# Attention and feed-forward in one kernel: low parts of the input weights to GpSimd, new ranks, whole batches in order, seven groups behind the attention

## The chip, the cores and the metric

The kernel runs on one core of one Trainium2 chip. The metric is the device time of one execution in microseconds (us). The kernel before was run three times: 585.23, 585.49 and 589.45 us, so its median is 585.49 us. The engines are called PE (matrix multiply), DVE (vector), ACT (scalar), POOL (GpSimd) and SP (it issues most DMAs). Each works through its own queue in the order in which the program was built, and waits at an instruction until what it needs is there.

## What is computed

The reference is an attention over 4 batches of 8 heads (576 positions, head width 64) with a recurrent memory, followed by a feed-forward layer on the 2304 x 512 result, all in float32:

```
scores = where(causal, -1e9, q @ k.T / sqrt(D))
a      = exp(scores - rowmax);  a /= a.sum + 1e-9
qp     = phi(q) = where(q > 0, q, exp(q) - 1) + 1
x      = g * (qp @ M_prev) / (qp . z_prev + 1e-6) + (1 - g) * (a @ v)      g = sigmoid(beta)
h      = x @ w_in                  # 2304 x 512 by 512 x 2048
out    = (s * relu(h)**2 + b) @ w_out
```

## The kernel before

**The three stages.** First comes the attention, in 16 pairs of heads (four pairs to a batch), then what is left of the first product (x @ w_in), then the second product, which is made with Strassen's seven products out of 256-wide quarters. To keep float32 accuracy every operand of a product is split into a high part (H) and a low part (L), and a product is three matmuls: H by H, H by L, L by H. Lines 494 to 496 are these three for the first product, 705 to 707 for the second.

**A pair of heads** goes through: scores on PE (line 322) into the banks `sb`; the row maximum on DVE with the mask added (329, `red`), which also moves the scores to SBUF; the exponential on ACT (335); the reciprocal of the sums on DVE (366, 367); ten scalings on POOL (341); transposes on PE (391) into the banks `tb`; copies of these banks on ACT and DVE (401 to 408); the product with V on PE (434); and at its end x is split into `xs`, high part on ACT (455) and low part on DVE (456). The query's feature map (272 to 286) runs on ACT, DVE and POOL beside it. All buffers of a pair exist twice, so two pairs are in flight.

**The weights w_in** come as float64 words in 20 pieces: 8 small ones (256 columns) and 12 large ones (512 columns). Each is made into float32 by one step on ACT (480) and three on DVE (481, 482, 484); POOL then writes the high part (486) and DVE subtracts it for the low part (487).

**The first product** is cut into groups: batch b by 128 columns of w_in, f = 0 to 15, twelve matmuls of 512 columns each. A group can run as soon as the batch's four pairs and its pieces of w_in are done. Groups of batches 0, 1 and 2 (48 of them) fill PE between the attention's steps; a ReLU on ACT (514) and a DMA to HBM (515) take each result out. Batch 3 and the 256 leftover columns of all batches (called batch 4) come behind the attention: there PE's results land in `hps`, one of 8 PSUM banks, go through the ReLU of line 500 into `r` and by DMA (501) to HBM.

**What sets the order.** Up to the end of the attention the order of every engine is written by a planner (`Plan`, lines 42 to 143): each step has an engine, an assumed cost and a rank, and of the steps that are ready the one of lowest rank goes first. On PE a group of the first product goes on until attention work has been ready for `HOLD` us or amounts to `WORK` us. Behind the attention the work is written step by step: `t_mm1` makes half a group, `tick` counts, and `later(n, ...)` hangs other work n ticks behind. That other work is the conversion of w_out in 16 pieces (`conv_u`, `t_u`, `split_u`, lines 604 to 634), the start of the second product's left operand (`g_load`, `g_make`, `operand`) and the ReLU with its DMA. A scheduler may still move these instructions on DVE, ACT and POOL.

## Time and profile before

| | before |
|---|---|
| three runs, us | 585.23, 585.49, 589.45 |
| profiled execution, us | 584.89 |
| its span, first to last instruction, us | 583.1 |
| PE busy | 546.6 us, 94% |
| ACT busy | 396.6 us, 68% |
| DVE busy | 367.9 us, 63% |
| POOL busy | 307.1 us, 53% |

The profiled execution's time is 1.8 us more than its span: that is what lies around the first and the last instruction. Its 584.89 us stand 0.6 us below the median. A busy share is an average over the stages, and it counts a slow or overlapped instruction as busy as well, so PE's 94% does not say that only 6% can be won. In the windows of the trace, a line gives for one stretch of the span the busy time of each engine with its instructions in brackets, then PE's granted clock (1.00 is 2.4 GHz, half of it 1.2 GHz) and the share and speed of the DMAs.

### The profile page before, as it was taken

Reading aid. Unit: us, or ns where it says so; the run is one execution under the profiler, and the core shown is the slowest. Engines: PE = TensorE matmul, PEld = TensorE weight load, DVE = VectorE, ACT = ScalarE, POOL = GpSimd, SP = SyncE. Lnnn points to the kernel's source line nnn. Section 1 sums busy time; section 2 is a strip of 40 time slices with the busy share of each in tenths; the row PEclk is TensorE's granted clock in tenths of the full one; section 3 lists DMA queues with packets and bytes.
Section 4 is the critical chain, followed back from the end, with each engine's and each line's share of the span. In section 5 each row is a group of like instructions: output and inputs, shape, how many; then the busy total and the mean of one; then the engine's idle time right before and its main releaser. Section 6 shows DMA issues by size and latency. Waiting matters only on the chain.

```text
span 583.1 us, 11806 instructions
## 1 busy us (share of the span) xinstructions
PE 546.6 (94%) x4309; PEld 462.5 (79%) x4309; DVE 367.9 (63%) x884; ACT 396.6 (68%) x846; POOL 307.1 (53%) x325
## 2 busy tenths in 40 slices
PE   6986996899989999999999999987999999999997
PEld 4755764577768777777778888876999999999997
DVE  4889898787752156453210389689657866695561
ACT  4898877667643278766632457958897779777940
POOL 2699778757752046554300000044786688668750
PEclk9799899799999999999999999997999999999999
DMA  6635566356623234331112876727344344444011
GB/s 185 191 117 157 154 202 202 121 165 205 194 85 129 91 97 130 105 119 60 51 59 90 315 228 208 261 110 241 131 136 144 121 142 142 139 124 139 28 38 37
DMA packets 53354, 81.52 MB, mean 140 GB/s; under 512 B 7216, under 2 KB 32816, under 8 KB 53296
## 3 DMA queue, kind: packets, MB, share of 16 engines
q1 hardware_dynamic: 52144, 79.19, 42.4%
q10 hardware_dynamic: 1152, 1.57, 0.7%
q8 instruction: 34, 0.56, 0.4%
q14 instruction: 24, 0.20, 0.1%
HBM read 57.15 MB, written 23.59 MB: 138 GB/s over the span
## 4 chain that ended last, share of the span: by engine, by line
PE 68%; ACT 8%; DVE 7%; POOL 7%; DMA 6%; issue 3%; SPq 0%; ACTq 0%; POOLq 0%; DVEq 0%
PE yps L707 10%; PE yps L705 10%; PE yps L706 10%; PE tb L494 7%; PE sb L434 7%; PE tb L496 6%; PE tb L495 6%; PE sb L322 6%; DMA r_d<-r 5%; POOL P L341 5%; PE tb L391 4%; ACT P L335 2%; DVE P L329 2%; DMA raw<-in_moe_w_out_dram 1%; ACT r L500 1%
## 5 line engine op out<-in xcount | busy, mean ns | idle before, releaser
L341 POOL TENSOR_SCALAR P<-P,sm,omg 128x192 f32<-128x192 f32 (+4 forms) x160 | 114.7, 735 | 71.5 <-DVE sm L367 45.2
L707 PE MATMUL yps<-bH,op 128*128 128x256 f32 x360 | 102.2, 284 | 4.2 <-DVE op L697 4.2
L706 PE MATMUL yps<-bL,op 128*128 128x256 f32 x360 | 102.2, 284 | 0.1
L705 PE MATMUL yps<-bH,op 128*128 128x256 f32 x360 | 102.2, 284 | 0.0
L335 ACT ACTIVATE P<-P,mn 128x64 f32<-128x64 f32 (+4 forms) x160 | 88.5, 561 | 18.8 <-DVE mn L329 18.8
L691 POOL TENSOR_TENSOR sum<-w0L 128x512 f32<-128x512 f32 x20 | 34.6, 1734 | 121.2 <-DVE stg L203 92.2
L329 DVE CUSTOM_DVE_ANT_0 P<-sb,mask 128x320 f32<-128x320 f32 (+4 forms) x160 | 69.4, 483 | 32.7 <-PE sb L322 31.8
L707 PEld LDWEIGHTS yps<-bH,op 128*128 128x128 f32 x360 | 68.9, 192 | 4.4 <-DVE op L697 4.4
L706 PEld LDWEIGHTS yps<-bL,op 128*128 128x128 f32 x360 | 68.8, 191 | 0.3 <-DVE bL L634 0.3
L705 PEld LDWEIGHTS yps<-bH,op 128*128 128x128 f32 x360 | 68.9, 191 | 0.2 <-ACT bH L633 0.2
L322 PE MATMUL sb<-qk 64*128 64x288 f32 (+4 forms) x384 | 62.9, 437 | 5.3 <-DVE mn L329 4.4
L391 PEld LDWEIGHTS tb<-ident,P 64*128 64x128 f32 x928 | 41.0, 143 | 31.4 <-POOL P L286 7.7
L391 PE MATMUL tb<-ident,P 64*128 64x64 f32 x928 | 47.5, 233 | 17.4 <-POOL P L341 5.0
L514 ACT ACTIVATE r<-tb 128x512 f32<-128x512 f32 x48 | 28.5, 594 | 46.0 <-PE tb L496 41.2
L322 PEld LDWEIGHTS sb<-qk 64*128 64x128 f32 x384 | 41.7, 200 | 18.5 <-DVE mn L329 7.5
L401 ACT COPY pt<-tb 128x512 f32<-128x512 f32 x64 | 34.4, 594 | 18.2 <-PE tb L391 18.1
L697 POOL TENSOR_TENSOR op<-w0L,op 128x512 fp32r<-128x512 f32 x30 | 41.6, 1407 | 4.9 <-ACT op L696 4.7
L696 ACT CAST op<-w0L 128x512 fp32r<-128x512 f32 x50 | 30.2, 614 | 18.5 <-PE yps L707 11.3
L705 PE MATMUL yps<-w0H,op 128*128 128x256 f32 x144 | 40.7, 283 | 0.0
L706 PE MATMUL yps<-w1H,op 128*128 128x256 f32 x144 | 40.7, 283 | 0.0
L707 PE MATMUL yps<-w0H,op 128*128 128x256 f32 x144 | 40.7, 283 | 0.0
L494 PE MATMUL tb<-xs,w0H 128*128 128x512 f32 x96 | 40.6, 422 | 0.0
(135 smaller groups left out, 1428.6 us busy)
## 6 DMA issues: line engine op xcount, KB each, us to landing
r_d<-r SPq DMA_DIRECT2D x60, 256.0 KB, 2.0
w0L<-r_d SPq DMA_DIRECT2D x20, 512.0 KB, 4.8
qk<-in_qk_t_dram SPq DMA_DIRECT2D x15, 576.0 KB, 4.1
raw<-in_moe_w_out_dram SPq DMA_DIRECT2D x16, 512.0 KB, 5.1
w1L<-r_d SPq DMA_DIRECT2D x16, 512.0 KB, 4.4
xa<-in_moe_w_in_dram SPq DMA_DIRECT2D x12, 512.0 KB, 4.4
qs<-in_q_rows_dram SPq DMA_DIRECT2D x16, 320.0 KB, 3.8
V<-in_vm_dram SPq DMA_DIRECT2D x16, 256.0 KB, 2.7
```

Source lines behind the costliest of these rows:

```text
L322: nc.tensor.matmul(SB[ps[j]][:, o:o + n], lhsT=qk[rs, 128 * i:128 * i + 128], rhs=qk[rs, S + 64 + c0:S + 64 + c0 + n], start=True, stop=Tr ...
L329: nc.vector.tensor_tensor_reduce(P[:, j, PB[i] + 64:PB[i] + 64 + n], SB[ps[j]][:, o:o + n], m, -SCALE, 3.0e38, ALU.add, ALU.min, mn[:, j, ...
L335: nc.scalar.activation(pt, pt, AF.Exp, scale=-1.0, bias=mn[:, j, i:i + 1], accum_out=sm[:, j, i:i + 1])
L341: nc.gpsimd.tensor_scalar(pt, pt, sm[:, j, i:i + 1], omg[:, h:h + 1], ALU.mult, ALU.mult)
L391: nc.tensor.transpose(TB[ps[h]][:, o[h]:o[h] + 64], P[rs, j, c:c + 128], ident[rs, rs], tile_position=(64 * h, 0))
L434: nc.tensor.matmul(t[64 * j:64 * j + 64, off:], lhsT=V[:, c, j], rhs=rhs, start=k == 0, stop=k == len(steps[0]) - 1, tile_position=(0, 64 ...
L494: nc.tensor.matmul(ps, lhsT=wH[:, p, fs], rhs=xs[:, 0], start=p == 0, stop=False)
L495: nc.tensor.matmul(ps, lhsT=wH[:, p, fs], rhs=xs[:, 1], start=False, stop=False)
L697: (nc.gpsimd if m in ONPOOL else nc.vector).tensor_sub(L, x, H.bitcast(F32))
L705: nc.tensor.matmul(ps, lhsT=H, rhs=BH, start=f == 0, stop=False)
L706: nc.tensor.matmul(ps, lhsT=H, rhs=BL, start=False, stop=False)
L707: nc.tensor.matmul(ps, lhsT=L, rhs=BH, start=False, stop=f == KF - 1)
```

## The change

- The low part of w_in (the subtraction of line 487) goes from DVE to POOL for the first 16 of the 20 pieces; the last four stay on DVE.
- Ranks: the row maxima (by `UR`), the copies of the transposes' banks (by `UC`) and the split of x (by `UX`) are ranked earlier, that is, ahead of other work on DVE and ACT; the pieces of w_in get earlier ranks (the largest falls from 20.8 to 16.2). `HOLD` and `WORK` change from 1.5 and 1.0 to 1.0 and 2.0.
- The groups of the first product go by whole batches: all 16 of batch 0, then all 16 of batch 1, then nine of batch 2. Before, eight of batch 0 came first, then eight of batch 1, and then the other halves.
- Seven groups of batch 2 (f = 9 to 15) run behind the attention, ahead of batches 3 and 4.
- There the ReLU works in pieces of 256 columns with three buffers of one kind; before, one buffer held 512 columns and another 256. The DMA of a piece goes on ACT's queue for batch 2 and on SP's for the rest; before, on ACT's for f below 4.
- The conversion of w_out gets other ticks (`CT`), and the first operands of the second product come six ticks sooner behind their start.

```diff
-    SWITCH, HOLD, WORK = 0.14, 1.5, 1.0
+    SWITCH, HOLD, WORK = 0.14, 1.0, 2.0
...
-    rpool = p1.enter_context(tc.tile_pool(name="rpool", bufs=1))
+    rpool = p1.enter_context(tc.tile_pool(name="rpool", bufs=3))
...
+    UR, UC, UX = 0.6, 0.5, 1.0
...
             for k, (i, o) in enumerate(tiles):
-                    add("DVE", RED[i], lambda i=i, j=j, o=o, ps=ps: red(i, j, o, ps), r + 0.1 + 0.01 * k,
+                    add("DVE", RED[i], lambda i=i, j=j, o=o, ps=ps: red(i, j, o, ps), r + 0.1 + 0.01 * k - UR,
...
             for h in range(2):
-                    r + 0.1, [("tp", g, k)], [("pt", u if k > 1 else 2, h, k)], give=[(ps, h, "T")])
+                    r + 0.1 - UC, [("tp", g, k)], [("pt", u if k > 1 else 2, h, k)], give=[(ps, h, "T")])
...
                 w = 0.16 + 0.00085 * (z - a)
-                add("ACT", w, lambda t=t, d=d: nc.scalar.copy(d[:, 0], t()), r0 + 2.3, [("av", g)], key(0))
+                add("ACT", w, lambda t=t, d=d: nc.scalar.copy(d[:, 0], t()), r0 + 2.3 - UX, [("av", g)], key(0))
-                    r0 + 2.3, [("av", g)] + key(0), key(1),
+                    r0 + 2.3 - UX, [("av", g)] + key(0), key(1),
...
         add("POOL", 0.8, lambda: nc.gpsimd.tensor_scalar(H, w, 1.0, 1.0, ALU.mult, ALU.mult), rank, [B_], [("WH", n)])
-        add("DVE", 0.8, lambda: nc.vector.tensor_sub(L, w, H.bitcast(F32)), rank, [B_, ("WH", n)], [("WL", n)])
+        low = ("POOL", 1.35, nc.gpsimd) if n < WP else ("DVE", 0.8, nc.vector)
+        add(*low[:2], lambda: low[2].tensor_sub(L, w, H.bitcast(F32)), rank, [B_, ("WH", n)], [("WL", n)])
...
     def mm1_out(b, f, ps):
-        r = rpool.tile([128, COLS[b]], F32, tag=f"r{b // B}", name="r")
-        nc.scalar.activation(r, ps, AF.Relu)
-        (nc.scalar if f < 4 else nc.sync).dma_start(r_d[b][:, f], r)
+        for o in range(0, COLS[b], 256):
+            r = rpool.tile([128, 256], F32, tag="r", name="r")
+            nc.scalar.activation(r, ps[:, o:o + 256], AF.Relu)
+            (nc.scalar if b == 2 else nc.sync).dma_start(r_d[b][:, f, o:o + 256], r)
...
-    FSPLIT = 8
-    MM = [(b, f) for r in (range(0, FSPLIT), range(FSPLIT, NF)) for b in range(2) for f in r] + [(2, f) for f in range(NF)]
-    STAGE = [b if m < FSPLIT or b == 2 else 1 for m, (b, f) in enumerate(MM)]
-    WB, WS = 12.0, 0.8
-    WRANK = [6.5, 6.6, 7.0, 7.2] + [9.0, 9.1, 9.2, 9.3] + [WB + WS * k for k in range(12)]
+    LEFT = 7
+    MM = [(b, f) for b in range(B - 1) for f in range(NF - LEFT * (b == 2))]
+    WP = 16
+    WRANK = [5.0, 6.6, 7.0, 7.2] + [9.0 + 0.2 * k for k in range(4)] + [10.0 + 0.2 * k for k in range(4)] + [
+        12.0 + 0.6 * k for k in range(8)]
...
             for m in range(len(MM)):
-                if STAGE[m] == g // NP:
+                if MM[m][0] == g // NP:
     with tc.manual_schedule():
-    MM = [(b, f, half) for f in range(NF) for b in (B, B - 1) for half in range(2)]
+    MM = [(2, f, half) for f in range(NF - LEFT, NF) for half in range(2)]
+    MM += [(b, f, half) for f in range(NF) for b in (B, B - 1) for half in range(2)]
     pa.close()
...
-    CT0, CT1 = 1, 3
+    CT = [1, 3, 6, 8, 10, 13] + [15 + 3 * k for k in range(10)]
...
-        later(CT0 + CT1 * i, conv_u, i)
+        later(CT[i], conv_u, i)
     while MM:
...
                 later(LT + i, g_make, 0, i)
-                later(max(LT + 4 + i, begin + CT0 + CT1 * (4 * i + 3) + 5 - clock[0]), late_b, i, 0)
+                later(max(LT + 4 + i, begin + CT[4 * i + 3] + 5 - clock[0]), late_b, i, 0)
-                later(LT + 14 + i, operand, 0, SEQ[i // 2], i % 2)
+                later(LT + 8 + i, operand, 0, SEQ[i // 2], i % 2)
```

The order of POOL near the seventh pair (the scalings of one pair and the feature map of the next; `w_106` and `w_107` are the two buffers of a piece of w_in, `w0H`, `w1H`, `w0L`, `w1L` its high and low parts). Before:

```order
L486 TENSOR_SCALAR w0H<-w_107 128x512
L341 TENSOR_SCALAR P_121<-P_121,sm_119,omg 128x576 x2
L486 TENSOR_SCALAR w0H<-w_106 128x512
L341 TENSOR_SCALAR P_122<-P_122,sm_120,omg 128x448
L486 TENSOR_SCALAR w0H<-w_107 128x512
L341 TENSOR_SCALAR P_122<-P_122,sm_120,omg 128x448
L341 TENSOR_SCALAR P_122<-P_122,sm_120,omg 128x192 x2
L276 TENSOR_TENSOR phr<-qs_114,z_112 128x640
L341 TENSOR_SCALAR P_122<-P_122,sm_120,omg 128x320 x2
L341 TENSOR_SCALAR P_122<-P_122,sm_120,omg 128x64 x2
L486 TENSOR_SCALAR w1H<-w_106 128x512
L286 TENSOR_TENSOR P_122<-qs_114,nrm_116 128x3x2x64
```

With the change:

```order
L487 TENSOR_SCALAR w0H<-w_106 128x512
L342 TENSOR_SCALAR P_121<-P_121,sm_119,omg 128x448
L489 TENSOR_TENSOR w0L<-w_106,w0H 128x512
L487 TENSOR_SCALAR w0H<-w_107 128x512
L342 TENSOR_SCALAR P_121<-P_121,sm_119,omg 128x192
L489 TENSOR_TENSOR w0L<-w_107,w0H 128x512
L342 TENSOR_SCALAR P_121<-P_121,sm_119,omg 128x192
L277 TENSOR_TENSOR phr<-qs_113,z_111 128x640
L487 TENSOR_SCALAR w1H<-w_106 128x512
L342 TENSOR_SCALAR P_121<-P_121,sm_119,omg 128x320
L489 TENSOR_TENSOR w1L<-w_106,w1H 128x512
L342 TENSOR_SCALAR P_121<-P_121,sm_119,omg 128x320
```

The low parts (489) now stand in POOL's queue, and the casts of the high parts (487) stand earlier by some pairs, both between the single scalings (342).

The order of PE where the attention's groups end and the work behind it begins (`tb` is a bank of the attention's stage, `hps` one of the stage behind it). Before:

```order
L496 MATMUL tb_101<-xs,w1L 128x512
L494 MATMUL tb_101<-xs,w1H 128x512
L495 MATMUL tb_101<-xs,w1H 128x512
L496 MATMUL tb_101<-xs,w1L 128x512
L494 MATMUL hps<-x_139,w0H 128x256
L495 MATMUL hps<-x_139,w0H 128x256
L496 MATMUL hps<-x_139,w0L 128x256
```

With the change:

```order
L498 MATMUL tb_100<-xs,w1L 128x512
L496 MATMUL tb_100<-xs,w1H 128x512
L497 MATMUL tb_100<-xs,w1H 128x512
L498 MATMUL tb_100<-xs,w1L 128x512
L496 MATMUL hps<-xs,w1H 128x512
L497 MATMUL hps<-xs,w1H 128x512
L498 MATMUL hps<-xs,w1L 128x512
```

The stage behind the attention now opens with batch 2 (`xs` with `w1H`), seven groups of it, where it opened with the leftover columns (`x`).

The order of DVE as the second product begins (`op` is a left operand, whose low part line 697, now 701, makes; `bL` are low parts of w_out; line 642, now 646, makes the last low parts into the place of `w1H`). Before:

```order
L695 TENSOR_TENSOR w0L<-w0L 128x4x128 x2
L697 TENSOR_TENSOR op<-sum,op 128x512
L634 TENSOR_TENSOR bL<-stg,bH 128x256
L642 TENSOR_TENSOR w1H<-late_3388,w0H 128x1024 x2
L634 TENSOR_TENSOR bL<-stg,bH 128x256
L642 TENSOR_TENSOR w1H<-late_3388,w0H 128x1024
L634 TENSOR_TENSOR bL<-stg,bH 128x768
L697 TENSOR_TENSOR op<-sum,op 128x512
L642 TENSOR_TENSOR w1H<-late_3388,w0H 128x1024
```

With the change:

```order
L638 TENSOR_TENSOR bL<-stg,bH 128x256 x2
L638 TENSOR_TENSOR bL<-stg,bH 128x768
L697 TENSOR_TENSOR w0L<-w0L 128x4x128
L699 TENSOR_TENSOR w0L<-w0L 128x4x128
L697 TENSOR_TENSOR w0L<-w0L 128x4x128
L701 TENSOR_TENSOR op<-sum,op 128x512
L699 TENSOR_TENSOR w0L<-w0L 128x4x128
L701 TENSOR_TENSOR op<-sum,op 128x512
L701 TENSOR_TENSOR op<-w0L,op 128x512 x2
L646 TENSOR_TENSOR w1H<-late_3290,w0H 128x1024 x4
```

The two low parts of `op<-sum` had three of the four instructions of line 642 and three of line 634 between them; now all of `bL` stands ahead of them, and line 642 behind the next operand as well.

## Rows read from the trace of the kernel before

**Rows 1.** The page, the chain that ended last: shares of the span by engine.

```profile
PE 68%; ACT 8%; DVE 7%; POOL 7%; DMA 6%; issue 3%; SPq 0%; ACTq 0%; POOLq 0%; DVEq 0%
```

**Rows 2.** Busy time by stretch (us): PE, PEld, DVE, ACT, POOL (instructions), granted clock, DMA.

```profile
64.60:92.20 27.60, 25.55 (x214) 18.24 (x214) 26.45 (x77) 21.31 (x61) 23.22 (x30) 1.00 0.67 201
64.60:131.90 67.30, 58.35 (x527) 41.60 (x527) 58.31 (x166) 49.31 (x133) 51.47 (x64) 0.95 0.57 171
131.90:302.90 171.00, 168.04 (x1311) 126.47 (x1311) 78.51 (x255) 102.66 (x262) 78.64 (x107) 1.00 0.35 112
302.90:322.20 19.30, 19.30 (x88) 16.00 (x87) 0.82 (x2) 4.29 (x8) 0.00 (x0) 1.00 0.22 82
392.40:402.00 9.60, 5.37 (x39) 4.76 (x39) 8.23 (x10) 7.78 (x16) 1.74 (x2) 0.87 0.81 277
402.00:579.00 177.00, 177.00 (x1474) 176.82 (x1473) 117.86 (x165) 134.53 (x192) 124.80 (x85) 0.99 0.36 113
420.00:560.00 140.00, 140.00 (x1182) 140.00 (x1181) 98.96 (x138) 114.91 (x163) 104.42 (x72) 1.00 0.37 118
```

**Rows 3.** Busy time by stretch of line 494 alone, PE and PEld: four such matmuls make a group.

```profile
64.60:131.90 67.30, 11.13 (x27) 4.94 (x27) 0.95 0.57 171
131.90:302.90 171.00, 57.26 (x139) 25.81 (x139) 1.00 0.35 112
```

**Rows 4.** Timeline of PE, 153 to 159 us: start, duration, engine, line.

```profile
153.31 0.50 PE L494 MATMUL tb<-xs,w0H 128*128 128x512 f32 x1
...
158.98 0.71 PE L391 MATMUL tb<-ident,P 64*128 64x64 f32 x16
```

**Rows 5.** Groups by line on POOL: out<-in, xcount | busy us, mean ns | idle before, releaser.

```profile
L341 POOL TENSOR_SCALAR P<-P,sm,omg 128x192 f32<-128x192 f32 (+4 forms) x160 | 114.7, 735 | 71.5 <-DVE sm L367 45.2 <-DVE omg L549 9.8 <-ACT P L335 4.0
...
L697 POOL TENSOR_TENSOR op<-w0L,op 128x512 fp32r<-128x512 f32 x30 | 41.6, 1407 | 4.9 <-ACT op L696 4.7
...
L276 POOL TENSOR_TENSOR phr<-qs,z 128x640 f32<-128x640 f32 x15 | 23.5, 1564 | 12.8 <-DVE qs L274 9.5 <-ACT P L335 2.4 <-DMA z<-in_z_prev_dram 0.8
L286 POOL TENSOR_TENSOR P<-qs,nrm 128x384 f32<-128x384 f32 (+1 forms) x30 | 23.1, 786 | 23.8 <-DVE nrm L282 14.9 <-PE tb L391 8.9
L486 POOL TENSOR_SCALAR w0H<-w 128x256 fp32r<-128x256 f32 (+1 forms) x12 | 5.9, 500 | 1.8 <-DVE w L484 1.8
L486 POOL TENSOR_SCALAR w1H<-w 128x512 fp32r<-128x512 f32 x8 | 5.7, 709 | 8.0 <-DVE w L484 6.4 <-DVE nrm L279 1.6
```

**Rows 6.** Groups by line on DVE: the conversion of w_in.

```profile
L484 DVE SCALAR_TENSOR_TENSOR w<-xa,w 128x512 uint32<-128x512 uint32 (+1 forms) x20 | 13.8, 696 | 0.0
L482 DVE SCALAR_TENSOR_TENSOR w<-xa,w 128x512 uint32<-128x512 uint32 (+1 forms) x20 | 13.0, 661 | 0.1
L487 DVE TENSOR_TENSOR w1L<-w,w1H 128x512 fp32r<-128x512 f32 x8 | 9.7, 1218 | 4.5 <-POOL w1H L486 4.5
L481 DVE TENSOR_SCALAR w<-w 128x512 uint32<-128x512 uint32 (+1 forms) x20 | 9.4, 476 | 0.2
```

**Rows 7.** Busy time by stretch of line 487 alone on DVE.

```profile
64.60:131.90 67.30, 9.61 (x10) 0.95 0.57 171
```

**Rows 8.** Timeline of PE at its two long stops behind the attention.

```profile
380.60 0.50 PE L494 MATMUL hps<-xs,w1H 128*128 128x512 f32 x1 [2.22 <-ACT r L500]
...
401.65 0.58 PE L707 MATMUL yps<-bH,op 128*128 128x256 f32 x1 [4.16 <-DVE op L697]
```

**Rows 9.** Timeline of DVE, 394 to 401 us: the low parts of the second operand.

```profile
394.25 0.69 DVE L697 TENSOR_TENSOR op<-sum,op 128x512 fp32r<-128x512 f32 x1 [1.36 <-ACT op L696]
...
400.92 0.68 DVE L697 TENSOR_TENSOR op<-sum,op 128x512 fp32r<-128x512 f32 x1
```

**Rows 10.** Groups by line on ACT: the ReLU behind the attention.

```profile
L500 ACT ACTIVATE r<-hps 128x256 f32<-128x256 f32 (+1 forms) x32 | 14.9, 488 | 20.0 <-DMA r_d<-r 16.2 <-PE hps L496 3.1 <-ACT r L500 0.5
```

**Rows 11.** The page, DMA issues: xcount, KB each, median us from issue to landing.

```profile
r_d<-r SPq DMA_DIRECT2D x12, 128.0 KB, 2.0
...
r_d<-r ACTq DMA_DIRECT2D x4, 128.0 KB, 5.6
```

More of the change, by code (lines that the diff above doesn't have):

```diff
@@ L584, in attention_moe_kernel @@
     RAW = [0, 1, 2, 3, 4, 5, 6, 7, 4, 5, 6, 7, 8, 6, 7, 8]
-    NR = 4
+    NRAW = 4
     NEXT = {n: (n + 4,) for n in range(9)} | {3: (), 4: (7, 8)} | {10: (13,), 11: (14,), 12: (15,)}
@@ L738, in attention_moe_kernel @@
     LT = 2
-    for i in range(NR):
+    for i in range(NRAW):
         load_u(i)
```

## Prediction

> **What bounds the kernel now.** I read the page first, then the busy times by stretch, cut where a batch or a stage ends, then the groups by line on POOL and DVE, and last the timelines of PE and DVE behind the attention. The chain of waits runs two thirds over PE and spreads the rest evenly over ACT, DVE, POOL and DMAs [rows 1], so no single engine can be relieved; one has to ask stage by stage what PE waits for. Four stretches matter, and the stretch table shows them [rows 2].
>
> From 64.6 us (the fourth pair, the last of batch 0, has its product with V) to 131.9 us (the eighth has it) DVE is busy for 58.3 of 67.3 us, a share of 0.87, POOL for 51.5 (0.765), and PE's clock is not at full throughout: nobody is full, the three wait for one another. From 131.9 to 302.9 us (the end of the last pair) PE is busy for 168.0 of 171.0 us at full clock and DVE for less than half: PE is the bound. From 302.9 to 322.2 us PE runs the last seven groups of batch 2 while DVE works for 0.8 us and POOL not at all. Behind that PE stops for 2.22 us for a ReLU on ACT, and, as the second product begins, for 4.16 us for an operand of DVE [rows 8].
>
> Two prices follow. Two groups back to back, 24 matmuls, take 158.98 - 153.31 = 5.67 us [rows 4], so a group is 2.83 us. In the stretch bound by PE there are 139 matmuls of line 494, a quarter of which is 34.5 groups, and in the one before 27, that is 6.5 groups [rows 3] (a matmul across a border counts twice). PE's share of a pair is then (168.0 - 34.5 x 2.83) / 8 = 8.80 us.
>
> **The change part by part.** The matmuls stay the same in number and size; only what PE waits for can change.
>
> *First 64.6 us.* No group can run there, and the order holds the same pairs and nearly the same pieces of w_in. I take nothing; an earlier row maximum may win a little, a piece of w_in more on POOL may cost as much. Both ends stay under 2 us.
>
> *From the fourth pair to the eighth.* In PE's order 12 groups now stand between these two points, before 6.5. PE's work there is 12 x 2.83 + 4 x 8.80 = 69.2 us; before it was 53.6. POOL's is four pairs of ten scalings (114.7 / 16 = 7.17), one product with z (1.57) and its share of the writes of the feature map (23.1 / 15 = 1.54), 10.28 each, so 41.1 us [rows 5]; 15 casts, nine at 0.50 and six at 0.71, 8.8 us [rows 5]; and 13 low parts. Their price is not in the trace. The nearest row is POOL's subtraction of the same shape and types in line 697, 1.41 us [rows 5]: eight large ones at 1.43 and five small ones at half of it and a little more, 0.75, give 15.2 us. If they went at DVE's price, 1.22 us [rows 6], it would be 13; at that of the product with z, 1.56, 17. Sum 65.1 us. DVE keeps three steps a piece, 0.48 + 0.66 + 0.70 = 1.84 us [rows 6]. Before, some ten pieces fell into the stretch, 18.4 us, with ten low parts of 9.6 us [rows 7], so the pairs themselves are 58.3 - 28.0 = 30.3. Now 15 pieces, 27.6 us, and the last four low parts, 4.9, make 62.8 us. So three engines have 69, 65 and 63 us to do, where the fullest had 58. The fullest of the stretch before reached 0.87; with that, PE needs 69.2 / 0.87 = 79.5 us, 12.2 more than before, and has 5.5 groups more behind it, worth 15.6 us. Gain: 3.4 us. The ends: PE without a gap, 69.2 us, gain 13.7; POOL as the bound at its own share of now, 65.1 / 0.765 = 85.1 us, loss 2.2. I stay with 0.87 because it is this stretch's own figure for a fullest engine among several that wait for one another.
>
> *One port rule.* Over 64.6 to 92.2 us DVE is busy for 26.45 of 27.6 us and POOL for 23.22 [rows 2], so at least 22 us of the two lie on top of each other. The Trainium skill, "Perfetto Trace Analysis", section "Optimizing Scalar/DVE Operations", says that GpSimd and DVE share a read port that a two-port DVE instruction holds alone, so that moving work from one to the other may not help. By that rule the 15.2 us would come back as time on DVE; by the row they run beside it. The sum goes by the row, the rule's result is a rival below.
>
> *From the eighth pair on.* 29 groups and eight pairs are left on PE either way, and PE was without work for only 3.0 us there [rows 2]. The cover stays: POOL needs 82 of some 150 us, DVE less than before, since the conversion is over by then. But the groups are cut more often by attention steps: counted in PE's order, 45 pieces instead of 39 to the end of the attention stage. The first matmul of a piece lasts 0.50 us [rows 4]; I take 0.2 us for a cut, 1.2 us in all (ends: 0, and 3 with 0.5 each), and the same 3.0 us of idle time.
>
> *The seven groups.* On PE they are merely put behind: 19.3 us either way [rows 2]. What they change is the time that the conversion of w_out has before the second product. Before, SP reached the loads of w_out only behind the last group's result, at 322 us; now the loads stand behind the attention's own last groups, and the seven groups run on top of the conversion. That gives DVE and ACT 19 us more. So the two stops should go. The second product's stop is seen in the order too: of the two low parts of `op<-sum`, made at 394.25 and 400.92 us [rows 9], the second no longer has lines 642 and 634 in front of it. The second product's 1512 matmuls (9 tiles, 7 products, 8 steps, 3 matmuls) take 579.0 - 392.4 = 186.6 us; at the pace of 420 to 560 us, 140 / 1182 = 0.118 us [rows 2], they would take 179.0. So 7.6 us hang on that stop, the slow clock behind it included (0.87 in that stretch), and 2.2 on the ReLU's: 9.8 us at most. I take 7, because PE may have to wait a little for the ReLU of one of the new groups; the ends are 0 and 9.8.
>
> *ReLU in halves.* The work on ACT grows by some microseconds (more and shorter instructions, 0.49 us in the mean now [rows 10]), under PE's cover as long as the eight banks don't run full.
>
> Sum against the profiled execution: 584.9 - 3.4 + 1.2 - 7 = 575.7 us. That execution is 0.6 us below the median of the runs, so I forecast **576.3 us**.
>
> **The rivals.**
>
> *PE runs full from the fourth pair.* The reds ranked first take the conversion out of the attention's way, and the waits fill with groups. Gain 13.7 instead of 3.4: 584.9 - 13.7 + 1.2 - 7 = 565.4, 566.0 as a median. For it: with groups at hand PE lost 3.0 in 171 us. Against: PE, POOL and DVE are now within 10% of each other.
>
> *The second stage gives nothing back.* The seven groups make 14 DMAs on ACT's queue while w_out is loaded, and such a DMA took 5.6 us to land there, against 2.0 on SP's [rows 11]. With three buffers a piece has its turn every (0.49 + 5.6) / 3 = 2.0 us, 14 pieces need 28 us where PE needs 19.3; ACT is then 9 us late, the conversion queued behind those ReLUs too, and the waits for the DMA of `r` (16.2 us now [rows 10]) grow. Then 584.9 - 3.4 + 1.2 = 582.7, 583.3 as a median.
>
> *The shared port.* DVE is held while POOL subtracts: 62.8 + 15.2 = 78.0 us, at 0.87 89.7, 22.4 more than before for 15.6 of groups. 584.9 + 6.8 + 1.2 - 7 = 585.9, 586.5 as a median: no change. Against it stands the overlap above.
>
> *POOL holds the scalings (slower).* The casts and low parts stand between the scalings, and each cast waits for DVE's third step, so the scalings behind it wait too, and the transposes and PE's groups behind those. If POOL's share falls to 0.70 by this, the stretch takes 65.1 / 0.70 = 93.0 us, 25.7 more for 15.6 of groups: 584.9 + 10.1 + 1.2 - 7 = 589.2, 589.8 as a median. It decides below a share of 0.73, where the 7 us from behind are eaten up; below 0.69 it is over 1% slower. For it: POOL idled 45.2 us for the reciprocals on DVE before its scalings [rows 5]. Against: those waits were short where it had much to do (0.84 from 64.6 to 92.2 us).
>
> **How the numbers follow.** My forecast has 0.42, PE full 0.18, nothing given back 0.16, the port 0.11, POOL slower 0.09, something else 0.04. About 1%, 5.9 us, can be told from no change. The forecast's own range is 569 to 582, some 0.85 of it below 579.6; with the case of a full PE and a little of the others that makes 0.58 for faster. Slower takes half of POOL's case and half of the unknown, 0.07. The rest, 0.35, is within 1%. The range from 564 to 588 leaves out the better half of the full PE, the worse half of POOL's and the unknown.
>
> **What would show it.** Right: between the fourth and the eighth pair 12 groups in some 80 us, PE's share there near 0.87; POOL's low parts at 1.4 us; the last pair near 294 us, with two groups behind it before the seven; no stop of 4 us as the second product begins, and that product in about 180 us. Wrong: PE idle before transposes for POOL over 12 us in the stretch, DVE's conversions longer than 0.48 to 0.70 us beside POOL's subtractions (the port), ACT's waits for `r` above 16 us with PE stopped for a ReLU.

## The result: 569.63 us, 16.8 us less than before

Run beside one another on one chip, the kernel before took 586.38 us (585.23 to 589.45) and the changed one 569.63 us (569.1 to 570.74, four runs): a ratio of 0.971, 95% interval 0.967 to 0.975. The profiled execution of the change took 569.1 us, its span 567.3, so 15.8 us of span have to be accounted for. The page of the changed kernel: span, busy time and share of the engines, PE's busy tenths and its granted clock in 40 slices, and the chain that ended last by engine.

```profile
span 567.3 us, 11900 instructions
...
PE 543.0 (96%) x4309; PEld 457.8 (81%) x4309; DVE 357.0 (63%) x868; ACT 398.4 (70%) x869; POOL 319.7 (56%) x341
...
PE   5987998999999999999999999999999999999996
...
PEclk9898998999999999999999999999999999999999
...
PE 64%; DVE 9%; POOL 9%; DMA 7%; ACT 7%; issue 3%; SPq 1%; ACTq 0%; POOLq 0%; DVEq 0%
```

PE is now busy for 96% of the span, at nine tenths or more from the eighth slice to the last but one, and the share of DVE and POOL in the chain [rows 1] has grown from 7% to 9% each, at the cost of PE's. The stretches that answer to [rows 2], cut where the fourth, the eighth and the last pair are done, where the attention's last group ends, and where the second product begins:

```profile
65.00:141.60 76.60, 69.54 (x573) 50.00 (x573) 65.40 (x163) 53.84 (x142) 66.56 (x73) 0.98 0.62 188
141.60:291.40 149.80, 149.43 (x1225) 109.18 (x1225) 64.37 (x234) 95.07 (x246) 73.27 (x103) 1.00 0.31 103
291.40:297.10 5.70, 5.70 (x25) 4.72 (x26) 0.82 (x2) 1.30 (x3) 0.00 (x0) 1.00 0.12 46
297.10:383.30 86.20, 86.00 (x469) 74.69 (x468) 55.75 (x110) 57.04 (x124) 8.30 (x6) 1.00 0.63 214
383.30:562.90 179.60, 179.60 (x1513) 179.47 (x1511) 119.99 (x168) 136.58 (x198) 121.54 (x84) 1.00 0.39 123
```

How many groups ran in the first two of them follows from line 496 alone, as in [rows 3] (PE, PEld; four such matmuls make a group):

```profile
65.00:141.60 76.60, 19.25 (x45) 8.56 (x45) 0.98 0.62 188
141.60:291.40 149.80, 47.49 (x113) 20.97 (x113) 1.00 0.31 103
```

One of the 45 starts at 141.53 us, right behind the eighth pair's last product with V, and is the first of the next group. So 11 groups ran between the fourth pair and the eighth, where the prediction reckoned with 12; 28 followed up to the last pair and two behind it, 41 in all. Before, one of the 27 in [rows 3] lies across the border in the same way, which leaves 6.5 groups.

| stretch | before, us | after, us | worth |
|---|---|---|---|
| to the fourth pair | 64.6 | 65.0 | +0.4 |
| fourth to eighth pair | 67.3 with 6.5 groups | 76.6 with 11 | +9.3 - 4.5 x 2.83 = -3.4 |
| eighth pair to the attention's last group, without the seven | 190.3 - 12.7 - 19.3 = 158.3 | 155.5 | -2.8 |
| the seven groups and the stage behind the attention | 19.3 + 70.0 = 89.3 | 86.2 | -3.1 |
| second product | 186.8 | 179.7 | -7.1 |
| what ends the span | 4.1 | 4.3 | +0.2 |

The sum is -15.8 us. In the seven groups, the stage and the second product PE stands still for 0.2 us in all: the two stops of [rows 8] are gone. Between the eighth pair and the attention's last group PE idled for 3.0 us before and for 0.4 us now. Behind the fourth pair only the second stretch still has gaps to speak of, 7.1 us. There PE is busy for 69.54 us and POOL for 66.56, shares of 0.91 and 0.87. The chain of waits within that stretch alone, by line, before and then with the change:

```profile
by line: PE sb L434 23.6%; POOL P L341 15.1%; PE tb L391 7.8%; PE tb L494 5.3%; DVE P L329 4.9%; PE sb L322 4.3%; POOL P L286 4.1%; DVE w L484 3.9%; DVE w0L L487 3.6%; PE tb L496 3.5%; issue 3.5%; DVE w L482 3.4%; PE tb L495 3.4%; DVE w L48
```

```profile
by line: POOL P L342 25.6%; POOL w0L L489 8.4%; issue 8.0%; DVE P L330 8.0%; POOL P L287 6.2%; POOL w0H L487 4.7%; PE sb L435 4.3%; DVE w L485 3.9%; POOL w1H L487 3.7%; DVE w L483 3.6%; DVE w L482 3.4%; POOL phr L277 2.6%; ACT P L336 2.3%; 
```

With the change POOL's lines make 51% of it: the scalings (342) a quarter, low parts (489) 8%, writes of the feature map (287) 6%, casts (487) 8%. Before, PE's line 434 came first with 24%, and the scalings had 15%. So POOL now has the largest part in this stretch, as near to full as DVE was before. The conversion's groups by line, which answer to [rows 5, 6] (out<-in, count | busy us, mean ns | idle before, releaser):

```profile
L342 POOL TENSOR_SCALAR P<-P,sm,omg 128x192 f32<-128x192 f32 (+4 forms) x160 | 113.1, 720 | 63.3 <-DVE sm L368 44.1 <-DVE omg L552 8.6 <-DVE sm L367 5.2
...
L483 DVE SCALAR_TENSOR_TENSOR w<-xa,w 128x512 uint32<-128x512 uint32 (+1 forms) x20 | 16.1, 807 | 0.2 <-DVE sm L368 0.2
...
L485 DVE SCALAR_TENSOR_TENSOR w<-xa,w 128x512 uint32<-128x512 uint32 (+1 forms) x20 | 14.3, 716 | 0.0
...
L482 DVE TENSOR_SCALAR w<-w 128x512 uint32<-128x512 uint32 (+1 forms) x20 | 10.8, 543 | 4.7 <-ACT w L481 4.7
...
L489 POOL TENSOR_TENSOR w0L<-w,w0H 128x256 fp32r<-128x256 f32 (+1 forms) x12 | 12.3, 1027 | 0.0
...
L489 POOL TENSOR_TENSOR w1L<-w,w1H 128x512 fp32r<-128x512 f32 x4 | 5.3, 1320 | 0.2
```

Large low parts cost 1.32 us on POOL, the mean of the four into `w1L` (taken: 1.43); the group above mixes eight small ones with four large. DVE's three remaining steps became longer: 807, 543 and 716 ns, where they were 661, 476 and 696. That is 0.233 us for each of 20 pieces, 4.7 us in all. Not all of it belongs to the subtractions on POOL. The three steps together take 1.83 us a piece in the profile of the kernel before, but 1.98 and 1.99 us in runs 7 and 12, which have the same low parts and the same order up to the eighth pair. With the change's order (the change and runs 1, 2, 3 and 11) they take 2.05 to 2.09 us, and 1.93 in run 4, which has all low parts on DVE. By these means some 0.14 us a piece, 2.8 us, goes with the low parts on POOL. The ReLU behind the attention, which answers to [rows 10]:

```profile
L503 ACT ACTIVATE r<-hps 128x256 f32<-128x256 f32 x62 | 22.0, 387 | 10.3 <-DMA r_d<-r 7.2 <-PE hps L498 2.5
```

It now waits for DMAs of `r` for 7.2 us, where it was 16.2, with twice the instructions.

### The profile page after: what moved, and what is told of

It reads as the page before. It is cut to its first block, busy times and chain, and to the rows that moved or that the text cites. A ratio compares the mean times of both kernels' runs of the same rounds, so it can differ in the third digit from the quotient of the medians.

```text
span 567.3 us, 11900 instructions
## 1 busy us (share of the span) xinstructions
PE 543.0 (96%) x4309; PEld 457.8 (81%) x4309; DVE 357.0 (63%) x868; ACT 398.4 (70%) x869; POOL 319.7 (56%) x341
## 4 chain that ended last, share of the span: by engine, by line
PE 64%; DVE 9%; POOL 9%; DMA 7%; ACT 7%; issue 3%; SPq 1%; ACTq 0%; POOLq 0%; DVEq 0%
PE yps L709 11%; PE yps L711 11%; PE yps L710 11%; PE tb L496 6%; PE sb L435 5%; PE sb L323 5%; PE tb L498 5%; PE tb L497 5%; DMA raw<-in_moe_w_out_dram 5%; POOL P L342 4%; PE tb L392 3%; DVE P L330 2%; ACT P L336 2%; POOL w0L L489 1%; DMA r_d<-r 1%
## 5 line engine op out<-in xcount | busy, mean ns | idle before, releaser
L342 POOL TENSOR_SCALAR P<-P,sm,omg 128x192 f32<-128x192 f32 (+4 forms) x160 | 113.1, 720 | 63.3 <-DVE sm L368 44.1
L336 ACT ACTIVATE P<-P,mn 128x64 f32<-128x64 f32 (+4 forms) x160 | 88.5, 562 | 24.1 <-DVE mn L330 23.9
L709 PE MATMUL yps<-bH,op 128*128 128x256 f32 x360 | 101.2, 281 | 0.0
L711 PE MATMUL yps<-bH,op 128*128 128x256 f32 x360 | 101.1, 281 | 0.0
L695 POOL TENSOR_TENSOR sum<-w0L 128x512 f32<-128x512 f32 x20 | 30.4, 1519 | 106.8 <-ACT w0L L675 82.8
L711 PEld LDWEIGHTS yps<-bH,op 128*128 128x128 f32 x360 | 67.9, 189 | 0.0
L709 PEld LDWEIGHTS yps<-bH,op 128*128 128x128 f32 x360 | 67.8, 188 | 0.0
L392 PEld LDWEIGHTS tb<-ident,P 64*128 64x128 f32 x928 | 39.3, 142 | 26.6 <-issue 8.1
L392 PE MATMUL tb<-ident,P 64*128 64x64 f32 x928 | 45.9, 232 | 10.9 <-POOL P L287 3.2
L517 ACT ACTIVATE r<-tb 128x512 f32<-128x512 f32 x41 | 24.3, 593 | 32.8 <-PE tb L498 28.7
L695 POOL TENSOR_TENSOR sum<-w1L 128x512 f32<-128x512 f32 x16 | 24.4, 1525 | 30.9 <-DVE op L701 26.8
```

Source lines behind the costliest of these rows:

```text
L336: nc.scalar.activation(pt, pt, AF.Exp, scale=-1.0, bias=mn[:, j, i:i + 1], accum_out=sm[:, j, i:i + 1])
L342: nc.gpsimd.tensor_scalar(pt, pt, sm[:, j, i:i + 1], omg[:, h:h + 1], ALU.mult, ALU.mult)
L392: nc.tensor.transpose(TB[ps[h]][:, o[h]:o[h] + 64], P[rs, j, c:c + 128], ident[rs, rs], tile_position=(64 * h, 0))
L695: nc.gpsimd.tensor_sub(x, y, A[{7: 21, 3: 11}[m]])
L709: nc.tensor.matmul(ps, lhsT=H, rhs=BH, start=f == 0, stop=False)
L711: nc.tensor.matmul(ps, lhsT=L, rhs=BH, start=False, stop=f == KF - 1)
```

## Experiments

Each kernel ran beside the kernel before on one chip. Times are medians; stretches are those of the profile. Beside these runs, on three chips, the kernel before took 584.8 to 586.6 us, so a difference from the change, which was not measured beside them, is good to some 2 us. Profiles of one and the same order differ too: up to the fourth pair the kernel before and runs 7 and 12 take 64.6 to 67.0 us, the change and runs 1, 2, 3 and 11 take 63.2 to 65.9, and from there to the eighth pair these five take 76.6 to 78.2.

**1. No groups behind the attention** (from the change).

```diff
-    LEFT = 7
+    LEFT = 0
```

> The changed kernel, but none of batch 2's groups behind the attention (LEFT 0 instead of 7); all else as changed. Theory (head start: the seven groups give the conversion of w_out 19 us before the second product, and that removes the two stops): the stops come back, the second product takes 183 to 187 us from its first matmul to its last instead of 179.7, the stage ahead of it loses 2 to 3 us; total 575 to 580. Rival (the ticks and the three r buffers removed the stops, the groups were merely moved): total 568.5 to 571, second product within 1 us of 179.7.

580.07 us (578.94 to 583.45), 10.4 us above the change. The attention was as fast (last pair at 290.8 us). Stretches behind it, the stage and the second product; then PE's one long stop, and DVE's instructions ahead of it:

```profile
315.40:386.20 70.80, 67.59 (x385) 58.99 (x384) 52.43 (x103) 49.04 (x104) 6.14 (x4) 1.00 0.69 232
386.20:573.40 187.20, 181.20 (x1513) 180.78 (x1511) 126.76 (x176) 140.60 (x205) 124.23 (x86) 0.98 0.38 119
```

```profile
394.97 0.58 PE L710 MATMUL yps<-bL,op 128*128 128x256 f32 x1 [6.00 <-DVE bL L638]
```

```profile
387.75 1.29 DVE L701 TENSOR_TENSOR op<-sum,op 128x512 fp32r<-128x512 f32 x2
388.95 5.63 DVE L646 TENSOR_TENSOR w1H<-late,w0H 128x1024 fp32r<-128x1024 f32 x3
394.51 1.61 DVE L638 TENSOR_TENSOR bL<-stg,bH 128x256 fp32r<-128x256 f32 x3
```

The stage loses 3.2 us to idle PE and the second product 6.0, of 187.2 against 179.6. The stop ends with a low part of w_out (638), which stands in DVE's queue behind 5.63 us of line 646. So without the seven groups on top of it the conversion is late again, and the scheduler puts it behind other work as well; the run doesn't part these two. The head start that the groups give is worth some 10 us. The theory held; its two stretches and the total came out at or just above the upper ends.

**2. The old ReLU buffers** (from the change; the DMA's queue stays by batch).

```diff
-    rpool = ... tc.tile_pool(name="rpool", bufs=3)
+    rpool = ... tc.tile_pool(name="rpool", bufs=1)
...
-        for o in range(0, COLS[b], 256):
-            r = rpool.tile([128, 256], F32, tag="r", name="r")
...
+        r = rpool.tile([128, COLS[b]], F32, tag=f"r{b // B}", name="r")
+        nc.scalar.activation(r, ps, AF.Relu)
+        (nc.scalar if b == 2 else nc.sync).dma_start(r_d[b][:, f], r)
```

> The changed kernel with the old buffers of r (one of 512 and one of 256 columns, a ReLU and a DMA per group; queues as in the change). With batch 2 in front, its seven groups share one buffer of 512 columns. Theory (head start): the ReLU gets late, but the banks and the 19 us carry it; total 569 to 573. Rival (the buffers removed the stops): PE stops for ReLUs, 5 us or more in the stage behind the attention, total 574 to 580.

574.73 us (573.63 to 574.93), +5.1. The ReLU's group by line on ACT:

```profile
L502 ACT ACTIVATE r<-hps 128x512 f32<-128x512 f32 (+1 forms) x39 | 19.6, 510 | 19.7 <-DMA r_d<-r 17.5 <-PE hps L498 2.1
```

The wait for DMAs of `r` is back at 17.5 us, and PE stops for 1.6 us for ACT before the second product, which takes 181.7 us. But 1.9 us of the loss lie before the eighth pair (143.5 against 141.6 us), where no `r` of this pool is in use. Some 3 us belong to the buffers. The total lies in the rival's range, but PE's stop is far from its 5 us: neither expectation held as it stood.

**3. The old ticks** (from the change).

```diff
-    CT = [1, 3, 6, 8, 10, 13] + [15 + 3 * k for k in range(10)]
+    CT = [1 + 3 * k for k in range(16)]
...
-                later(LT + 8 + i, operand, 0, SEQ[i // 2], i % 2)
+                later(LT + 14 + i, operand, 0, SEQ[i // 2], i % 2)
```

> The changed kernel with the old ticks: the conversion of w_out every third half group, the first operands 14 ticks behind their start instead of 8. Theory (head start): within 1.5 us of the changed kernel, 568.5 to 571.5, second product within 1.5 us of 179.7. Rival (the ticks did it): the stop at the start of the second product comes back, 573 to 577.

569.09 us (568.1 to 569.84): no effect. With seven groups of cover the ticks don't matter, as the theory had it.

**4. All low parts of w_in on DVE** (from the change).

```diff
-    WP = 16
+    WP = 0
```

> The changed kernel with all low parts of w_in on DVE (WP 0). Theory (DVE is relieved where it was the fullest): DVE gets some 10 to 14 us back between the fourth and the eighth pair, where it is busy for 65 of 77 us now; that stretch grows by 4 to 8 us, total 573 to 578. Rival (the order of the groups filled PE, and POOL is as full as DVE was): within 1.5 us, 568 to 571.5.

577.14 us (575.43 to 577.97), +7.5. Fourth to eighth pair:

```profile
65.30:157.90 92.60, 81.20 (x646) 57.81 (x648) 80.26 (x215) 63.48 (x167) 69.99 (x85) 0.94 0.57 171
```

92.6 us with 13 groups instead of 76.6 with 11: 16.0 us more, of which the two groups are worth 5.7. The theory's total is right, its 4 to 8 us for the stretch are too few. DVE is busy for 80.3 us, a share of 0.87 as in the kernel before. The attention's groups end at 306.0 us, 8.9 later. With the pieces this early, low parts on DVE cost 7.5 us. The conversion's steps on DVE in this run:

```profile
L485 DVE SCALAR_TENSOR_TENSOR w<-xa,w 128x512 uint32<-128x512 uint32 (+1 forms) x20 | 14.1, 707 | 0.0
L483 DVE SCALAR_TENSOR_TENSOR w<-xa,w 128x512 uint32<-128x512 uint32 (+1 forms) x20 | 13.9, 705 | 0.0
L482 DVE TENSOR_SCALAR w<-w 128x512 uint32<-128x512 uint32 (+1 forms) x20 | 10.4, 522 | 0.3 <-ACT w L481 0.2
```

**5. No earlier ranks** (from the change).

```diff
-    UR, UC, UX = 0.6, 0.5, 1.0
+    UR, UC, UX = 0.0, 0.0, 0.0
```

> The changed kernel with the three rank offsets at zero (UR, UC, UX), so that row maxima, bank copies and the split of x stand where their old ranks put them. Theory (the ranks take the conversion out of the attention's way, and made the stretch from the fourth to the eighth pair shorter than forecast): the eighth pair 3 to 7 us later, total 572 to 577. Rival (the low parts alone did it): within 1.5 us, 568 to 571.

575.17 us (574.93 to 576.62), +5.5.

```profile
65.00:151.30 86.30, 75.54 (x587) 53.57 (x585) 68.45 (x176) 57.18 (x146) 69.64 (x78) 0.94 0.56 173
```

The stretch takes 86.3 us, 9.7 more, with 12 groups instead of 11 (the one more is worth 2.8 us), and with neither DVE (0.79) nor POOL (0.81) as full as in the change. The groups end 6.2 us later. That is what the three offsets are worth together; the run doesn't part them.

**6. The old order of the groups** (from the change, seven groups still behind the attention).

```diff
-    MM = [(b, f) for b in range(B - 1) for f in range(NF - LEFT * (b == 2))]
+    MM = [(b, f) for r in (range(0, 8), range(8, NF)) for b in range(2) for f in r] + [(2, f) for f in range(NF - LEFT)]
+    STAGE = [b if m < 8 or b == 2 else 1 for m, (b, f) in enumerate(MM)]
...
-                if MM[m][0] == g // NP:
+                if STAGE[m] == g // NP:
```

> The changed kernel with the groups in the old order (eight of batch 0, eight of batch 1, then the other halves, then nine of batch 2). Theory (whole batches give PE 12 groups instead of at most 8 to put between the fourth and the eighth pair): up to 4 groups, 11.3 us, move behind the eighth pair and the stretch shortens by less than that, so the attention ends 2 to 6 us later, total 571 to 576. Rival (POOL and DVE set that stretch, PE's filling is only taken from later): within 1.5 us, 568 to 571.

583.24 us (581.77 to 587.14), +13.6, a ratio of 0.998 to the kernel before. Both expectations missed.

```profile
65.00:145.40 80.40, 66.42 (x539) 47.33 (x537) 65.91 (x168) 53.22 (x140) 67.40 (x75) 0.89 0.57 173
```

With eight groups instead of 11 the stretch got longer, not shorter: 80.4 us, with PE idle for 14.0 and a granted clock of 0.89. Its length is therefore not PE's work divided by a share: the three groups that PE does meanwhile in the change are free. DVE (65.9 us) and POOL (67.4) have as much to do as in the change. Why it is 3.8 us longer still isn't shown: PE waits for POOL's lines 342 and 287 for 9.0 us before its transposes, where the change has 3.8, but PE's own matmuls for the pairs, at the lower clock, also take 5.4 us more (66.4 - 8 x 2.83 = 43.8 us, in the change 69.5 - 11 x 2.83 = 38.4). Three groups fewer cost 3 x 2.83 = 8.5 us later on, and PE idles for 2.2 us there instead of 0.4; the groups end 14.4 us later.

**7. Seven groups behind the attention alone** (from the kernel before).

```diff
-    MM = ... + [(2, f) for f in range(NF)]
+    MM = ... + [(2, f) for f in range(NF - 7)]
...
-    MM = [(b, f, half) for f in range(NF) for b in (B, B - 1) for half in range(2)]
+    MM = [(2, f, half) for f in range(NF - 7, NF) for half in range(2)]
+    MM += [(b, f, half) for f in range(NF) for b in (B, B - 1) for half in range(2)]
```

> The kernel before with only the seven groups of batch 2 moved behind the attention; old ranks, low parts, ticks and r buffers. Theory (the head start removes the stops of the second product by itself; without the new r buffers some 3 us of it are lost): second product 179.5 to 183 us instead of 186.8, total 577 to 582. Rival (it needs the buffers and the ticks): second product 184 to 188, total 584 to 588.

577.31 us (576.75 to 580.61), a ratio of 0.989 (0.984 to 0.995), 7.5 us below the kernel before beside it. The profile, whose time is 580.61 us, is the slowest of its four executions.

```profile
306.40:392.50 86.10, 86.10 (x471) 74.75 (x469) 55.15 (x112) 55.13 (x103) 8.03 (x6) 1.00 0.58 201
392.50:574.70 182.20, 180.01 (x1513) 179.60 (x1512) 121.64 (x168) 137.66 (x198) 119.99 (x84) 1.00 0.39 124
```

Without any of the other parts the stage has no idle PE, and the second product has one stop of 2.18 us, for a ReLU: this kernel has the old buffers, and its ReLU waits 24.1 us for DMAs of `r`. The two buffer results (2 and 7) fit together.

**8. Low parts on POOL alone** (from the kernel before).

```diff
-        add("DVE", 0.8, lambda: nc.vector.tensor_sub(L, w, H.bitcast(F32)), rank, [B_, ("WH", n)], [("WL", n)])
+        low = ("POOL", 1.35, nc.gpsimd) if n < 16 else ("DVE", 0.8, nc.vector)
+        add(*low[:2], lambda: low[2].tensor_sub(L, w, H.bitcast(F32)), rank, [B_, ("WH", n)], [("WL", n)])
```

> The kernel before with only the low parts of the first 16 pieces on POOL. Theory (DVE was the fullest engine up to the eighth pair, so 14 us less on it shorten that stretch by themselves): attention 4 to 9 us shorter, total 577 to 582. Rival (alone it shifts the waits to POOL, and only with the new ranks and the new order of groups does PE find work): within 2 us of before, 584 to 588.

581.14 us (579.47 to 585.28), a ratio of 0.995 (0.992 to 0.998), 3.7 us less. Fourth to eighth pair:

```profile
66.90:125.60 58.70, 51.17 (x499) 37.66 (x499) 45.68 (x141) 44.67 (x125) 56.02 (x66) 0.94 0.57 184
```

58.7 us with 5.5 groups, before 67.3 with 6.5: 5.8 us better there. But the fourth pair came at 66.9 us, 2.3 later (as in runs 7 and 12: 66.8 and 67.0), and from the eighth pair on 1.9 us were lost, so the attention's last group ends at 320.6 us, 1.6 sooner than before and not 4 to 9. Another 2.0 us come from less idle PE in the stage behind it, where no low part of w_in is made. The total lies in the theory's range, its path only in part.

**9. The first four pieces' low parts on DVE, all others on POOL** (from the change).

```diff
-        low = ("POOL", 1.35, nc.gpsimd) if n < WP else ("DVE", 0.8, nc.vector)
+        low = ("POOL", 1.35, nc.gpsimd) if n >= 4 else ("DVE", 0.8, nc.vector)
```

> The changed kernel with the low parts of the first four pieces back on DVE and those of the last four on POOL as well. Theory (in the second to fourth pair POOL is full, 0.96 to 1.00, and DVE at 0.76 to 0.96, so the first four low parts cost there what they save later): the fourth pair 1 to 3 us sooner, total 566 to 569. Rival (the first pairs are set by ACT and by the chain of one pair): within 1.5 us, 568 to 571.

575.81 us (575.2 to 576.15), +6.2: the theory failed. The fourth pair came 1 us sooner (64.0), which is within what one and the same order varies by. POOL had 81.10 us to do up to the eighth, 14.5 more than in the change, and that came 85.0 us later at a share of 0.95, with 12 groups. The planner also deals the whole order anew after any such edit, so small ones can't be read one by one.

**10. Ranks twice as early** (from the change).

```diff
-    UR, UC, UX = 0.6, 0.5, 1.0
+    UR, UC, UX = 1.2, 1.0, 2.0
```

> The changed kernel with the three rank offsets doubled (1.2, 1.0, 2.0). Theory (the offsets work by putting attention ahead of the conversion, and at 0.6 to 1.0 it stands ahead already): within 2 us, 567.5 to 571.5. Rival (more of it helps on): 563 to 567. A loss of over 2 us would say that the conversion is now too late for the groups.

573.3 us (572.57 to 575.04), +3.7.

```profile
65.10:141.20 76.10, 66.26 (x564) 48.23 (x562) 68.27 (x160) 53.58 (x136) 72.18 (x82) 0.98 0.60 189
```

As long as the stretch of the change (76.1 us), but with ten groups, one fewer, which costs 2.8 us later; PE also idles for 1.4 us instead of 0.4 behind the eighth pair. This fits a conversion that comes too late for the groups, as the expectation has it for a loss.

**11. Four groups behind the attention** (from the change).

```diff
-    LEFT = 7
+    LEFT = 4
```

> The changed kernel with four groups behind the attention instead of seven, a head start of 11 us instead of 20. Theory (the head start is a matter of degree: at none the stops cost 10.5 us, at seven groups nothing, and DVE's order already had both low parts of the second operand in front at none): a part of the stops comes back, second product 180 to 184 us, total 570 to 575. Rival (four are enough): 568 to 570.

571.62 us (568.63 to 576.54), not to be told from the change.

```profile
306.20:384.90 78.70, 78.14 (x433) 67.94 (x431) 57.95 (x110) 54.30 (x116) 8.49 (x6) 1.00 0.65 220
384.90:564.80 179.90, 179.86 (x1512) 179.67 (x1512) 122.22 (x168) 136.79 (x200) 122.09 (x84) 1.00 0.39 125
```

0.6 us idle in the stage and none in the second product: four groups are already cover enough, as the rival had it. The gain isn't in proportion to their number.

**12. Whole batches alone** (from the kernel before).

```diff
-    MM = [(b, f) for r in (range(0, FSPLIT), range(FSPLIT, NF)) for b in range(2) for f in r] + [(2, f) for f in range(NF)]
-    STAGE = [b if m < FSPLIT or b == 2 else 1 for m, (b, f) in enumerate(MM)]
+    MM = [(b, f) for b in range(3) for f in range(NF)]
+    STAGE = [b for b, f in MM]
```

> The kernel before with only the groups in whole batches (16 of batch 0, 16 of batch 1, 16 of batch 2). Theory (whole batches pay only when the pieces of w_in for f above 7 come early; here they still come from rank 12 to 20.8, so batch 0's second half waits for them and batch 1's first half waits behind it in line): no gain or a loss, total 584 to 592. Rival (whole batches give 13 us by themselves, as their removal from the changed kernel cost): total 571 to 578.

586.23 us (582.59 to 589.14), a ratio of 1.001 (0.998 to 1.004): no change. The same edit is worth 13.6 us within the change (run 6). Sixteen groups of batch 0 need all 20 pieces of w_in, and here these come no sooner: up to the eighth pair (133.7 us) the trace has 6.5 groups, as before [rows 3]. There is nothing more to put into the gaps. (The profile, of 589.14 us, is the slowest of its ten executions.)

**Together.** Added to the kernel before one at a time, three parts give 7.5 + 3.7 + 0 = 11.2 of the 16.8 us. Taken out of the change one at a time, they cost 10.4 + 7.5 + 13.6, and the ranks 5.5 more, 37 us. The parts in the attention need one another; the seven groups stand almost by themselves. `HOLD`, `WORK` and the ranks of w_in were not tried by themselves, and each of these figures is good to some 2 us. None of these kernels beat the change; run 3 is level with it.

## Why the prediction was right, and where its sizes were off

The direction and the order of size held: 569.63 us lies inside 564 to 588, 6.7 us below the forecast of 576.3. The forecast was 4.0 us too high behind the eighth pair, where a gain came in place of a loss, and 3.2 at the two stops; some 0.5 us elsewhere went the other way.

- **First 64.6 us, nothing:** +0.4 us, right; one and the same order varies by more.
- **Fourth to eighth pair, gain 3.4:** it was 3.4, by luck. The prediction put 12 groups there and the trace has 11, so the groups' worth was 2.8 us too high, and the stretch was 2.9 us shorter than the 79.5 that it gave. PE's 69.54 us agree with 69.2 by chance as well: by the prediction's own prices 11 groups make 11 x 2.83 + 35.2 = 66.3 us, and the other 3.2 us are the pairs' own matmuls, which take longer in this stretch than in the later one that their price came from (before, too: 58.35 us where it worked out 53.6). POOL's 66.56 for 65.1 hides that 33 scalings and not 40 fell there, at 0.93 us in the mean and not 0.72.
- **The share of 0.87:** the rule "PE needs 69.2 / 0.87" has the wrong form. It gives 76.2 us for 11 groups, near the 76.6 measured. But for run 6, with PE's need at 8 x 2.83 + 35.2 = 57.8 us, it gives 66.5 us, and it took 80.4; for the 12 groups of run 5 it gives 79.5, and it took 86.3. Nor is 0.87 a constant of the engines that *make* the pairs. The fullest of them reaches it before and in run 4 (DVE) and in the change (POOL), but 0.81 in run 5, 0.84 in run 6 and 0.95 in runs 8, 9 and 10.
- **Behind the eighth pair, loss 1.2:** it was a gain of 2.8. The cuts cost next to nothing: PE's share of a pair is 8.8 us there before and after. What failed is the term "the same 3.0 us of idle time", which fell to 0.4. Why is open: it is 1.4 us in run 4 and 2.2 in run 6, so no single part explains it.
- **The two stops, gain 7:** 7.1 us in the second product and 3.1 in the stage, 10.2, where 9.8 was the upper end. The discount for late ReLUs had no cause: run 2 puts back the old buffers and gets the late ReLU back, so the small pieces removed it. Runs 1 and 7 show that the seven groups alone do most of this.
- **PE full (566.0):** the nearest of all by the number, 3.6 us off, but not by its mechanism. Its 13.7 was four times what came between the fourth and the eighth pair, where PE still idles for 7.1 us.
- **Nothing given back (583.3):** fell. It reckoned with 5.6 us for each DMA on ACT's queue; the 14 took 4.2 us (median), ACT's waits for `r` went down to 7.2 us, and PE waited 0.2 us for a ReLU.
- **The shared port (586.5):** the mechanism is there, as the last section shows, at some 2.8 us by the mean durations of DVE's steps and not at the 15.2 it was given. The sign that the prediction set down for it, DVE's conversion steps above 0.70 us beside POOL's subtractions, did appear. Its argument against, that DVE and POOL are both busy for 22 us of one stretch, proves little, since a step that waits for the other engine counts as busy too. The move paid all the same: 7.5 us by run 4, and by run 8 1.6 us in the attention.
- **POOL holds the scalings (slower):** its place was right, its price not. POOL has half of the chain in the stretch, but its share is 0.87, far from the 0.73 below which it would have decided. In run 9, where it has 14.5 us more to do, the whole costs 6.2 us.

## What to carry to other kernels

Where several engines feed one another, the big engine's sum does not give the length of a stretch, and work that it can do meanwhile can be free: ask how much of it can be made ready. How full the fullest feeding engine gets is no constant to reckon with (0.81 to 0.95 here). And count the work between two points in the trace before you trust a sum that agrees: two errors cancelled here. A few independent groups placed on top of a preparation phase buy the head start that the new timing of that phase alone did not give (run 1), and a few are enough (run 11). Parts of an edit that need one another show nothing when added alone, so take them out of the whole one at a time too.

## What was not expected of the hardware

Two stretches of the timelines of the changed kernel, DVE and then POOL (start, duration, engine, line): the second conversion step, which reads two tensors from SBUF, beside POOL's subtraction, which does so too.

```profile
88.62 0.68 DVE L483 SCALAR_TENSOR_TENSOR w<-xa,w 128x512 uint32<-128x512 uint32 x1
...
97.41 1.65 DVE L483 SCALAR_TENSOR_TENSOR w<-xa,w 128x512 uint32<-128x512 uint32 x1
...
115.27 1.74 DVE L483 SCALAR_TENSOR_TENSOR w<-xa,w 128x512 uint32<-128x512 uint32 x1
...
119.42 1.65 DVE L483 SCALAR_TENSOR_TENSOR w<-xa,w 128x512 uint32<-128x512 uint32 x1
```

```profile
88.63 1.79 POOL L489 TENSOR_TENSOR w0L<-w,w0H 128x512 fp32r<-128x512 f32 x1
...
97.04 1.47 POOL L489 TENSOR_TENSOR w0L<-w,w0H 128x512 fp32r<-128x512 f32 x1
...
115.18 1.29 POOL L489 TENSOR_TENSOR w1L<-w,w1H 128x512 fp32r<-128x512 f32 x1
...
119.09 1.43 POOL L489 TENSOR_TENSOR w1L<-w,w1H 128x512 fp32r<-128x512 f32 x1
```

Where DVE began first (88.62 us) it took its usual 0.68 us, and POOL's subtraction 1.79 instead of some 1.3. Where POOL was under way (97.04, 115.18 and 119.09 us), DVE's step took 1.65 to 1.74 us and ended 0.54 to 0.55 us after POOL's, some 0.1 us less than a whole step of its own: it did nearly all of its work after POOL had ended. So in these rows the two take turns, and whoever comes second waits. Line 482, which reads one tensor, can wait as well: at 78.43 us it took 0.94 us and ended 0.29 us after a subtraction that POOL had begun at 78.35 us. Line 483 has the largest part of what DVE's steps gained in length, 0.146 of 0.233 us a piece. The trace of the kernel before already had such a case in the stretch that the prediction took for running side by side, a step of 256 columns that takes 0.41 us at 25.82 us, beside POOL's product with z:

```profile
74.19 1.78 DVE L484 SCALAR_TENSOR_TENSOR w<-xa,w 128x256 uint32<-128x256 uint32 x1
```

```profile
73.96 1.72 POOL L276 TENSOR_TENSOR phr<-qs,z 128x640 f32<-128x640 f32 x1
```

The Trainium skill, "GPSIMD Engine Reference", section "1. Specifications", states this contention for DVE instructions in a two-port mode or with two SBUF inputs; these rows agree, for two inputs. By its "Perfetto Trace Analysis", section "Optimizing Scalar/DVE Operations", moving work between the two engines might not help; run 4 measured that within the change it does, by 7.5 us, for all that the turns cost.
